# Attention and feed-forward block on one Trainium2 core: the first chunk's output product in half blocks, the third batch moved, the end's additions reordered

## The chip, the core and the metric

The kernel runs on one core of a Trainium2 chip. TensorE (PE) multiplies, VectorE (DVE), ScalarE (ACT) and GpSimd (POOL) work element by element, and DMAs are issued from the queues of SyncE (SP), ACT and POOL. POOL's queue holds its sums and the issues of all loads, in one order. The metric is device time: 554.34 us, the median of three runs (554.24 to 554.39).

## What is computed

For 8 batches, 8 heads, 1024 positions and 64 values a head, keys and values are first projected along the sequence to 64 rows; then attention, then a gated feed-forward layer on the 8192 rows of 512:

```
k_proj = einsum('ks,bhsd->bhkd', E, k);  v_proj = einsum('ks,bhsd->bhkd', F, v)
attn = softmax(q @ k_proj^T / 8);        x = attn @ v_proj, heads side by side: 8192 x 512
out  = (silu(x @ w_gate) * (x @ w_val)) @ w_out          # 512 -> 1536 -> 512
```

## The kernel before, in words

The 8192 rows are 16 chunks of 512, two for each batch. The main loop (L849) has 192 iterations t = 12 c + f: chunk c, block f of 128 of the 1536 inner columns. An iteration is `f_g` (four matmuls of 512 columns, ACT's tanh), `f_v` (four more, and two operations on DVE that leave a block of hT, the inner activations), then what the table `late` holds for t. Around them run two *slots*, 2t behind `f_g` and 2t+1 behind the rest of the iteration. The dictionary `slots`, written out by hand in `place` (L651) and around it, puts the attention of the coming batches there. Every engine works in the order in which this code issues, so the tables set the order on PE, ACT, DVE, POOL and SP alike.

The steps of the attention of batch b, by their short names:

- `load_q`, `load_k`, `load_v`: DMAs from POOL's queue, float32 to bf16; q in two halves (ch 0 and 1). Within a slot the loads go first (L826).
- `u_KV` (or `u_K1`, `u_V1` for batch 1): the projections, PE into tile kvp, then copies. `u_KT`: keys transposed into the tile BD. `u_V1` and `u_KT` copy on DVE.
- `u_TD`: a transposing DMA on SP, qTd from qb. `u_S`: scores sc from qTd and BD (L353), exp on ACT into ee. `u_R`: sums and reciprocals on DVE. `u_N`: POOL divides, AAd from ee and rr (L383).
- `u_AD`: a transposing DMA on SP, AT from AAd (L338). Four `u_N` make one AAd. `u_PV`: pv from AT (L410), copied to xT, the feed-forward's input.

For batch 1 the scores stand in slots 35 to 38 and 41 to 44, `u_AD` in 41 and 47, the first four `u_PV` in 44, 45, 46 and 46. For batch 2 `u_KV` stands in slot 56, the first `u_TD` in 57, the scores in 62, 65 and so on to 83; its loads are issued in slots 43 (K, V), 44 and 45 (the halves of q). Later batches have the same steps at other distances.

The output product hT x w_out of a chunk has two forms. Chunk 0 uses the plain one, `f_y` (L492): 4 x 12 matmuls of 512 columns, in twelve parts laid into iterations 16 to 23. Chunks 1 to 15 use seven products of half blocks (Strassen-Winograd style), `f_m` (L604): for each of two row groups p seven products m = 3, 4, 5, 2, 1, 6, 7 of six matmuls of 256 columns, from sums of quarters of hT (`h_sum`, tiles hs1 to hs7) and of w_out (`w_sum`, tiles ws1 to ws7, made once). Their results are put together by `m_34` (ACT copies to xs, POOL adds into tt), `m_52` (ACT copies to ysb), `m_16` (DVE adds, POOL subtracts, L594) and `m_7` (DVE adds, SP stores). hs5 and hs2 are summed on POOL, block by block, in the second half of each chunk; hs1, hs6 and hs7 on DVE, in one operation each (L547, 128x1536) in the next chunk; the five `w_sum` on DVE in iterations 18 to 22.

PSUM banks come from rings of two (a, g, v) and two single banks y and z. While `ring["wide"]` is true (chunks 0 and 1) the attention's ring a takes bank z as a third one.

The last chunk has its own ending, `f_m_last` (L616): products 3, 6 and 4 of both row groups, then 5 and 2 with three DVE operations after each, then products 1 of both (into banks z1[0], z1[1]) and products 7 into the same banks, which DVE must have emptied by L640 before.

Of the kernel before, what the change touches and what calls it, by code (L numbers as in the profile page):

```python
# [10 lines left out]
ALU = mybir.AluOpType  # L11
AX = mybir.AxisListType
BF16 = mybir.dt.bfloat16
FP32 = mybir.dt.float32
# [6 lines left out]
DM = H * D  # L21
DFF = 1536
P = 128
# [3 lines left out]
NFT = DFF // P  # L27
# [11 lines left out]
def kernel(  # L39
# [155 lines left out]
    def u_V1(b, at="a"):  # L195

        t = bank(at, [P, NPAIR, D], FP32, "kvp")
        src = vb[b][:].rearrange("p (a c) j d -> p a c j d", c=2)
        for j in range(NJ):
            for c in range(2):  # L200
                nc.tensor.matmul(
                    out=t[64 * c : 64 * c + 64],
                    lhsT=FT[:, j, :],
                    rhs=src[:, :, c, j, :],
                    start=(j == 0),
                    stop=(j == NJ - 1),
                )
        for c in range(2):
            rows = slice(64 * c, 64 * c + 64)
            nc.vector.tensor_copy(out=BDV[b % 2][rows, :, rows], in_=t[rows])  # L210

    def u_V0(p0, p1, at):

# [42 lines left out]
    def u_KT(b, at="a", prs=(0, NPAIR)):  # L256

        t = bank(at, [P, NPAIR, KP], FP32, "kTp")
        for pr in range(*prs) if b > 1 else ():
            nc.tensor.matmul(
                out=t[:, pr, :],
                lhsT=ks[b % 2][:, 2 * pr : 2 * pr + 2, :].rearrange("p h d -> p (h d)"),
                rhs=ident_bf[:, 0:KP],
                start=True,
                stop=True,
            )
        for g in range(2) if b < 2 else ():  # L270
            turn_ksp(t, b, g)
        bd = BD[b % 2][:].rearrange("p (a c) k -> p a c k", c=2)
        for c in range(2):
            src = t[64 * c : 64 * c + 64, slice(*prs)]
            nc.vector.tensor_copy(out=bd[0:64, slice(*prs), c, 0:64], in_=src)
            nc.vector.tensor_copy(out=bd[64:128, slice(*prs), c, 64:128], in_=src)

    def u_KT0(prs, ats, engs):

# [207 lines left out]
            out=hT[c][:, f, :], in0=s1[:], scalar=0.5, in1=ps[:], op0=ALU.mult, op1=ALU.mult  # L487
        )

    yy = {}  # L490

    def f_y(c, n):  # L492

        i, part = divmod(n, 3)
        if part == 0:
            yy[c] = bank("y", [P, DM], FP32, "yps")
        for f in range(4 * part, 4 * part + 4):
            nc.tensor.matmul(
                out=yy[c][:],
                lhsT=hT[c][:, f, i * P : (i + 1) * P],  # L500
                rhs=wo[:, f, :],
                start=(f == 0),
                stop=(f == NFT - 1),
            )
        if part == 2:
            ysb = y_pool.tile([P, 2, DM], FP32, name="ysb", tag="ysb")
            nc.scalar.copy(out=ysb[:, 0], in_=yy[c][:])
            nc.sync.dma_start(out=rows_of(c)[:, i, :], in_=ysb[:, 0])

    def rows_of(c):  # L510
        b, ch = divmod(c, CH)
        return out[b * S : (b + 1) * S, :].rearrange("(p c j) d -> p c j d", c=CH, j=4)[:, ch]

    def quarter(t, half, x):
        return t[:, HF * half : HF * (half + 1), HC * x : HC * (x + 1)]

    def w_sum(m):

        (a, b), op = {
            1: (((0, 0), (1, 1)), ALU.add),  # L520
            3: (((0, 1), (1, 1)), ALU.subtract),
            4: (((1, 0), (0, 0)), ALU.subtract),
            6: (((0, 0), (0, 1)), ALU.add),
            7: (((1, 0), (1, 1)), ALU.add),
        }[m]
        nc.vector.tensor_tensor(out=ws[m][:], in0=quarter(wo, *a), in1=quarter(wo, *b), op=op)

    hs = {}

# [86 lines left out]
    def f_m_last(c):  # L616

        xx[c, 0], xx[c, 1] = m_bank("y"), m_bank("g")
        z6 = m_bank("a")
        z1 = [m_bank("av"[p]) for p in range(2)]  # L620
        for p in range(2):
            m_mm(c, p, 3, xx[c, p][:, 0], start=True)
        for p in range(2):
            m_mm(c, p, 6, z6[:, p], start=(p == 0))
        for p in range(2):
            m_mm(c, p, 4, xx[c, p][:, 1])
            m_34(c, p)
        for p in range(2):
            m_mm(c, p, 5, xx[c, p][:, 0])
            m_mm(c, p, 2, xx[c, p][:, 1])  # L630
            m_52(c, p)
            d, ysb = tt[c, p], yo[c, p]
            nc.vector.tensor_tensor(out=d[:, 1], in0=d[:, 0], in1=ysb[:, 2], op=ALU.subtract)
            nc.vector.tensor_tensor(out=d[:, 0], in0=d[:, 0], in1=ysb[:, 1], op=ALU.subtract)
            nc.vector.tensor_tensor(out=d[:, 1], in0=d[:, 1], in1=z6[:, p], op=ALU.add)
        for x in (1, 0):
            for p in range(2):
                m_mm(c, p, (7, 1)[x], z1[p][:, 0], start=(x == 1))
                ysb = yo[c, p]
                nc.vector.tensor_tensor(out=ysb[:, 3 * x], in0=tt[c, p][:, x], in1=z1[p][:, 0], op=ALU.add)  # L640
                (nc.sync, nc.scalar)[p].dma_start(
                    out=rows_of(c)[:, p + 2 * x, :], in_=ysb[:, 2 * x : 2 * x + 2].rearrange("p x d -> p (x d)")
                )


    slots = defaultdict(list)

    def put(s, fn, *a):
        slots[s].append((fn, a))

    def place(b):  # L651
        s0 = 48 * (b - 1)
        if b == 1:
            put(22, u_TD, 1, 0)
            put(29, u_K1, 1)
            put(32, u_KT, 1)
            put(40, u_V1, 1)
            sa = (35, 36, 37, 38, 41, 42, 43, 44)
            put(41, u_AD, 1, 0)
            put(30, u_TD, 1, 1)  # L660
            put(47, u_AD, 1, 1)
            sp = (44, 45, 46, 46, 66, 67, 68, 69)
        else:
            put(s0 + (8 if b == 2 else 0), u_KV, b)
            put(s0 + (11 if b == 2 else 3), u_KT, b)
            o = 14 if b == 2 else 6
            put(s0 + (9 if b == 2 else -6), u_TD, b, 0)
# [16 lines left out]
    with tc.manual_schedule():  # L684
# [131 lines left out]
            place(b)  # L816
        for b in range(2, B):
            s0 = 48 * (b - 1) - (20 if b == 3 else 24)
            at = (43, 43, 44, 45) if b == 2 else (s0, s0 + 2, s0 + 4, s0 + 6)
            put(at[0], load_k, b)  # L820
            put(at[1], load_v, b)
            put(at[2], load_q, b, 0)
            put(at[3], load_q, b, 1)
# [3 lines left out]


        late = defaultdict(list)
        for n in range(NFT):  # L830
            late[NFT + 4 + (2 * n + 1) // 3].append((f_y, 0, n))
        for m, f in ((3, 6), (4, 7), (6, 8), (7, 9), (1, 10)):
            late[NFT + f].append((w_sum, m))
        for c in range(1, NC):
            for f in range(HF):
                for m in (5, 2):
                    late[c * NFT + HF + f].append((h_sum, c, m, f, f + 1))
            if c == NC - 1:
# [51 lines left out]
```

## Time and profile before

| | |
|---|---|
| median of three runs | 554.34 us |
| the profiled execution's own time | 554.06 us |
| its span, first to last instruction | 552.3 us |
| PE busy | 537.3 us (97%) |
| DVE, POOL, ACT busy | 414.1, 294.5, 233.3 us |
| 512-column matmuls of f_g and f_v | some 190 us each |
| POOL's half sums hs, 128x256 (L547) | x180, 120.6 us, mean 691 ns |
| DVE's sums hs (L547), 128x1536 for the most part | x49, 46.1 us, mean 946 ns |
| loads: q half, K, V, issue to landing | median 18.1, 9.9, 14.8 us |
| transposing DMAs qTd and AT, issue to landing | median 6.0 and 4.2 us |

The profile is of one execution, so the times of single instructions are set against 554.06 and 552.3, not against the median. "x" is the number of instructions. Matmuls overlap: a duration of 379 ns for 512 columns holds the tail of the pipeline, while the next one starts 216 ns after. A wait of PE is named by what ended it. An idle engine other than PE costs nothing by itself; it does if PE, later, waits for what it makes.

### The profile page before, as it was taken

The page shows a single profiled execution, that of the slowest core. Times are in us where ns is not written, and L with a number is a line of the kernel's source. Part 1 is how long each engine was busy: PE and PEld are TensorE (multiplying, and loading weights), DVE is VectorE, ACT ScalarE, POOL GpSimd, SP SyncE. Part 2 cuts the span into 40 slices and gives each one's busy share as a digit, 9 for nine tenths or more (in the row PEclk, how much of TensorE's full clock was granted, in tenths as well). Part 3 has the DMA queues.
Part 4 walks back from the last instruction along what each step waited for, and adds up shares of the span by engine and source line. Part 5 has one row for each costly group of instructions (what it writes and reads, how often), then busy time and mean ns, then how long its engine had stood idle before and what let it go on. Part 6 is the DMA issues. An engine that isn't in the chain of part 4 may idle for free. (4 is left out here: it accounts for less than half of the span.)

```text
span 552.3 us, 9270 instructions
## 1 busy us (share of the span) xinstructions
PE 537.3 (97%) x3438; PEld 317.9 (58%) x3500; DVE 414.1 (75%) x699; ACT 233.3 (42%) x416; POOL 294.5 (53%) x364
## 2 busy tenths in 40 slices
PE   7999999999999999999999999999999999999996
PEld 4654545566565655566556655566656565555565
DVE  3787896878597875979579785788859786676883
ACT  3564453353445333443425434344244533433331
POOL 7851493467617934377534855268461763526171
PEclk9999999999999999999999999999999999999999
DMA  9999969929932598038941299214990212110013
GB/s 205 192 197 190 162 142 194 160 72 139 211 76 73 104 189 170 1 77 145 206 108 39 64 170 195 71 39 92 179 209 17 74 47 72 39 40 31 8 39 115
DMA packets 111630, 62.87 MB, mean 114 GB/s; under 512 B 65888, under 2 KB 102752, under 8 KB 111584
## 3 DMA queue, kind: packets, MB, share of 16 engines
q0 software_dynamic: 43952, 29.49, 37.5%
q1 hardware_dynamic: 66800, 31.20, 25.4%
q10 hardware_dynamic: 832, 1.57, 0.9%
q8 instruction: 27, 0.44, 0.3%
q14 instruction: 19, 0.16, 0.1%
HBM read 60.29 MB, written 16.78 MB: 140 GB/s over the span
## 5 line engine op out<-in xcount | busy, mean ns | idle before, releaser
L462 PE MATMUL vps<-xT,wv 128*128 128x512 bf16 (+1 forms) x759 | 195.0, 377 | 2.5 <-DMA wv<-in_moe_w_val_dram 0.8
L462 PE MATMUL gps<-xT,wg 128*128 128x512 bf16 (+1 forms) x729 | 191.6, 377 | 1.9
L474 ACT ACTIVATE th<-gps 128x512 f32<-128x512 f32 x191 | 114.1, 598 | 164.7 <-PE gps L462 153.9
L481 DVE SCALAR_TENSOR_TENSOR s<-th,gps 128x512 f32<-128x512 f32 x191 | 129.2, 676 | 67.5 <-ACT th L474 66.2
L547 POOL TENSOR_TENSOR hs<-hT 128x256 bf16<-128x256 bf16 x180 | 120.6, 691 | 57.9 <-DVE hT L486 57.2
L486 DVE SCALAR_TENSOR_TENSOR hT<-s,vps 128x512 bf16<-128x512 f32 x192 | 132.1, 688 | 20.4 <-PE gps L462 0.5
L462 PEld LDWEIGHTS <-wv 128*128 128x128 bf16 x776 | 73.9, 98 | 84.3 <-issue 3.0
L564 PEld LDWEIGHTS <-hs 128*128 128x128 bf16 x900 | 88.0, 98 | 36.7 <-issue 3.3
L462 PEld LDWEIGHTS <-wg 128*128 128x128 bf16 x776 | 74.1, 98 | 55.9 <-issue 0.6
L383 POOL TENSOR_TENSOR AAd<-ee,rr 128x512 bf16<-128x512 f32 x56 | 58.4, 1043 | 55.7 <-issue 33.6
L594 POOL TENSOR_TENSOR tt<-tt,ysb 128x512 f32<-128x512 f32 x28 | 35.5, 1268 | 71.7 <-DVE tt L593 71.7
L564 PE MATMUL yps<-ws,hs 128*128 128x256 bf16 x540 | 68.6, 272 | 1.5 <-DVE ysb L640 1.2
L583 POOL TENSOR_TENSOR tt<-xs 128x256 f32<-128x256 f32 x30 | 29.4, 981 | 51.3 <-ACT xs L581 51.2
L150 ACT CAST xT<-pv 128x512 bf16<-128x512 f32 (+1 forms) x63 | 36.4, 581 | 46.3 <-PE pv L410 44.3
L368 DVE TENSOR_REDUCE zz<-ee 128x8 f32<-128x512 f32 x64 | 43.3, 677 | 11.1 <-ACT ee L357 11.0
L564 PE MATMUL yps<-ws,hT 128*128 128x256 bf16 x360 | 48.8, 273 | 0.0
L564 PE MATMUL yps<-wo,hs 128*128 128x256 bf16 x360 | 48.6, 273 | 0.1
L547 DVE TENSOR_TENSOR hs<-hT 128x1536 bf16<-128x1536 bf16 (+1 forms) x49 | 46.1, 946 | 0.1
L357 ACT ACTIVATE ee<-sc 128x512 f32<-128x512 f32 x64 | 38.1, 598 | 18.5 <-PE sc L353 16.1
L564 PEld LDWEIGHTS <-hT 128*128 128x128 bf16 x360 | 35.2, 98 | 16.0
L581 ACT COPY xs<-yps 128x512 f32<-128x512 f32 x30 | 17.6, 585 | 30.6 <-PE yps L564 30.5
L588 ACT COPY ysb<-yps 128x512 f32<-128x512 f32 x30 | 17.6, 585 | 24.9 <-PE yps L564 21.6
(100 smaller groups left out, 318.0 us busy)
## 6 DMA issues: line engine op xcount, KB each, us to landing
out_dram<-ysb SPq DMA_DIRECT2D x28, 512.0 KB, 2.7
qb<-in_q_dram POOLq DMA_DIRECT2D x14, 512.0 KB, 18.1
kb<-in_k_dram POOLq DMA_DIRECT2D x7, 1024.0 KB, 9.9
vb<-in_v_dram POOLq DMA_DIRECT2D x7, 1024.0 KB, 14.8
wo<-in_moe_w_out_dram POOLq DMA_DIRECT2D x2, 768.0 KB, 21.4
out_dram<-ysb SPq DMA_DIRECT2D x6, 256.0 KB, 2.2
kraw<-in_k_dram ACTq DMA_DIRECT2D x2, 512.0 KB, 4.8
qb<-in_q_dram POOLq DMA_DIRECT2D x4, 256.0 KB, 7.9
```

The lines of the kernel that those rows point to most:

```text
L150: (nc.scalar.copy if eng is nc.scalar else eng.tensor_copy)(out=out, in_=in_)
L357: nc.scalar.activation(out=e[:].rearrange("p h j k -> p (h j k)"), in_=ps[:].rearrange("p a k -> p (a k)"), func=AF.Exp, scale=scale,)
L368: nc.vector.reduce_sum(out=z[:], in_=e[:], axis=AX.X)
L383: eng.tensor_tensor(out=a.rearrange("p j h k -> p h j k"), in0=ee.pop((b, u))[:], in1=rr.pop((b, u))[:].unsqueeze(3).to_broadcast([P, 4, 2 ...
L462: nc.tensor.matmul(out=ps[:, ts], lhsT=(wg, wv)[w][:, kt, f * P : (f + 1) * P], rhs=x[:, kt, ts], start=(kt == 0), stop=(kt == NKT - 1),)
L474: nc.scalar.activation(out=th[:], in_=ps[:], func=AF.Tanh, scale=0.5)
L481: nc.vector.scalar_tensor_tensor(out=s1[:], in0=th[:], scalar=1.0, in1=g[:], op0=ALU.add, op1=ALU.mult)
L486: nc.vector.scalar_tensor_tensor(out=hT[c][:, f, :], in0=s1[:], scalar=0.5, in1=ps[:], op0=ALU.mult, op1=ALU.mult)
L547: eng.tensor_tensor(out=hs[c, m][:, fs, :], in0=quarter(hT[c], *a)[:, fs], in1=quarter(hT[c], *b)[:, fs], op=op,)
L564: nc.tensor.matmul(out=ps, lhsT=lhsT, rhs=ws[m][:, f, :] if rhs is None else rhs, start=(start and f == 0), stop=(f == HF - 1), skip_group ...
L583: nc.gpsimd.tensor_tensor(out=t[:, 0], in0=xs[:, 0], in1=xs[:, 1], op=ALU.add)
L594: nc.gpsimd.tensor_tensor(out=t[:], in0=t[:], in1=yo[c, p][:, 1:3], op=ALU.subtract)
```

## The change

Four things are changed together.

1. Chunk 0 takes the seven products too; `f_y` goes. The fourteen parts stand in iterations 18 to 23, two or three in each. Their sums go to three engines: hs5 and hs2 block by block on POOL in iterations 6 to 11; hs6 on POOL in 12, hs1 on DVE in 13, hs7 on POOL in 14. The sum ws6 is made on POOL in iteration 15, ws3, ws4, ws1 and ws7 on DVE in 16, 17, 18 and 20. Bank z leaves the attention's ring from iteration 19 on (before, from 24).
2. Batch 2's steps from `u_KV` to the last score and the last `u_AD` come two slots later (its `u_TD` and `u_PV` stay). Its loads are issued in slots 40 (first half of q), 42 (K), 43 (V) and 45 (second half).
3. The copies of `u_V1`, and for batch 1 those of `u_KT`, go from DVE to ACT.
4. In `f_m_last` the additions of z6 come ahead of products 5 and 2, and one of the four subtractions goes behind the additions that empty z1.

The diff, without the removed `f_y`:

```diff
@@ u_V1
-            nc.vector.tensor_copy(out=BDV[b % 2][rows, :, rows], in_=t[rows])
+            nc.scalar.copy(out=BDV[b % 2][rows, :, rows], in_=t[rows])
@@ u_KT
-            nc.vector.tensor_copy(out=bd[0:64, slice(*prs), c, 0:64], in_=src)
-            nc.vector.tensor_copy(out=bd[64:128, slice(*prs), c, 64:128], in_=src)
+            for lo in (0, 64):
+                copy(nc.scalar if b == 1 else nc.vector, bd[lo : lo + 64, slice(*prs), c, lo : lo + 64], src)
@@ w_sum
-    def w_sum(m):
+    def w_sum(m, eng=nc.vector):
...
-        nc.vector.tensor_tensor(out=ws[m][:], in0=quarter(wo, *a), in1=quarter(wo, *b), op=op)
+        eng.tensor_tensor(out=ws[m][:], in0=quarter(wo, *a), in1=quarter(wo, *b), op=op)
@@ f_m_last
+        for p in range(2):
+            step(tt[c, p][:, 1], tt[c, p][:, 0], z6[:, p], add)
         for p in range(2):
             m_mm(c, p, 5, xx[c, p][:, 0])
             m_mm(c, p, 2, xx[c, p][:, 1])
             m_52(c, p)
-            d, ysb = tt[c, p], yo[c, p]
-            nc.vector.tensor_tensor(out=d[:, 1], in0=d[:, 0], in1=ysb[:, 2], op=ALU.subtract)
-            nc.vector.tensor_tensor(out=d[:, 0], in0=d[:, 0], in1=ysb[:, 1], op=ALU.subtract)
-            nc.vector.tensor_tensor(out=d[:, 1], in0=d[:, 1], in1=z6[:, p], op=ALU.add)
+        d, ysb = [tt[c, p] for p in range(2)], [yo[c, p] for p in range(2)]
+        step(d[0][:, 1], d[0][:, 1], ysb[0][:, 2], sub)
+        step(d[0][:, 0], d[0][:, 0], ysb[0][:, 1], sub)
+        step(d[1][:, 1], d[1][:, 1], ysb[1][:, 2], sub)
         for x in (1, 0):
             for p in range(2):
                 m_mm(c, p, (7, 1)[x], z1[p][:, 0], start=(x == 1))
-                nc.vector.tensor_tensor(out=ysb[:, 3 * x], in0=tt[c, p][:, x], in1=z1[p][:, 0], op=ALU.add)
+                step(ysb[p][:, 3 * x], d[p][:, x], z1[p][:, 0], add)
...
+            if x:
+                step(d[1][:, 0], d[1][:, 0], ysb[1][:, 1], sub)
@@ place
-            put(s0 + (8 if b == 2 else 0), u_KV, b)
-            put(s0 + (11 if b == 2 else 3), u_KT, b)
-            o = 14 if b == 2 else 6
+            put(s0 + (10 if b == 2 else 0), u_KV, b)
+            put(s0 + (13 if b == 2 else 3), u_KT, b)
+            o = 16 if b == 2 else 6
@@ loads of batch 2 (slots of K, V, q first half, q second half)
-            at = (43, 43, 44, 45) if b == 2 else (s0, s0 + 2, s0 + 4, s0 + 6)
+            at = (42, 43, 40, 45) if b == 2 else (s0, s0 + 2, s0 + 4, s0 + 6)
@@ late
-        for n in range(NFT):
-            late[NFT + 4 + (2 * n + 1) // 3].append((f_y, 0, n))
-        for m, f in ((3, 6), (4, 7), (6, 8), (7, 9), (1, 10)):
+        for m, f in ((3, 4), (4, 5), (1, 6), (7, 8)):
             late[NFT + f].append((w_sum, m))
-        for c in range(1, NC):
+        late[NFT + 3].append((w_sum, 6, nc.gpsimd))
+        for c in range(NC):
...
-                for i, m in enumerate((1, 6, 7)):
-                    late[(c + 1) * NFT + 1 + i].append((h_sum, c, m, 0, HF, nc.vector))
-                for n, f in enumerate((0, 1, 2, 3, 4, 4, 5, 6, 7, 8, 9, 10, 10, 11)):
+                for m, f, eng in ((6, 0, nc.gpsimd), (1, 1, nc.vector), (7, 2, nc.gpsimd)) if c == 0 else (
+                    (1, 1, nc.vector), (6, 2, nc.vector), (7, 3, nc.vector)
+                ):
+                    late[(c + 1) * NFT + f].append((h_sum, c, m, 0, HF, eng))
+                fs = (6, 6, 7, 7, 8, 8, 9, 9, 9, 10, 10, 11, 11, 11) if c == 0 else (0, 1, 2, 3, 4, 4, 5, 6, 7, 8, 9, 10, 10, 11)
+                for n, f in enumerate(fs):
                     late[(c + 1) * NFT + f].append((f_m, c, n))
@@ main loop
-            ring["wide"] = c < 2
+            ring["wide"] = t < NFT + 7
```

More of the change, by code (lines that the diff above doesn't have):

```diff
@@ L488, in f_v @@
         )
[L490 to L508, printed above, removed]
     def rows_of(c):
@@ L627, in f_m_last, with step @@
             m_34(c, p)
+        add, sub = ALU.add, ALU.subtract
+        def step(o, i0, i1, op):
+            nc.vector.tensor_tensor(out=o, in0=i0, in1=i1, op=op)
+        for p in range(2):
+            step(tt[c, p][:, 1], tt[c, p][:, 0], z6[:, p], add)
         for p in range(2):
@@ L638, in f_m_last @@
                 m_mm(c, p, (7, 1)[x], z1[p][:, 0], start=(x == 1))
-                ysb = yo[c, p]
-                nc.vector.tensor_tensor(out=ysb[:, 3 * x], in0=tt[c, p][:, x], in1=z1[p][:, 0], op=ALU.add)
+                step(ysb[p][:, 3 * x], d[p][:, x], z1[p][:, 0], add)
                 (nc.sync, nc.scalar)[p].dma_start(
-                    out=rows_of(c)[:, p + 2 * x, :], in_=ysb[:, 2 * x : 2 * x + 2].rearrange("p x d -> p (x d)")
+                    out=rows_of(c)[:, p + 2 * x, :], in_=ysb[p][:, 2 * x : 2 * x + 2].rearrange("p x d -> p (x d)")
                 )
+            if x:
+                step(d[1][:, 0], d[1][:, 0], ysb[1][:, 1], sub)
     slots = defaultdict(list)
```

## The prediction

> **What bounds the kernel.** Read first the busy shares, then what TensorE (PE) waits for, then its timeline at each place the change touches.
>
> ```profile
> PE 537.3 (97%) x3438; PEld 317.9 (58%) x3500; DVE 414.1 (75%) x699; ACT 233.3 (42%) x416; POOL 294.5 (53%) x364
> ```
> ```profile
> PE yps L564 <- DVE ysb L640: 1.2, 1, 1.2
> PE kvp L162 <- DMA vb<-in_v_dram: 0.9, 1, 0.9
> ...
> PE sc L353 <- DMA qTd<-qb: 0.4, 1, 0.4
> ```
>
> PE is the bound: after the first 30 us almost nothing holds it but these three waits (us in total, times, longest), and all three are edited. So each edit is worth what it does to PE's stream. Matmuls start 0.216 us apart at 512 columns (4 in 0.865) and 0.109 apart at 256 (12 in 1.31); a wait's real loss is a little more than the idle shown, because the last matmul's tail counts as busy.
>
> **The output product of chunk 0.** It removes 48 matmuls of 512 columns, 48 x 0.216 = 10.38 us, and adds 2 x 7 x 6 = 84 of 256, 84 x 0.109 = 9.17: on paper 1.21 us less. But it also moves them. Three parts of the old product (L498, 3 x 0.865 = 2.59 us) stood before the first score of batch 1; all the new ones stand behind it. Here is that score (sc), with the wait that the table doesn't show:
>
> ```profile
> 57.97 1.89 PE L498 MATMUL yps<-wo,hT 128*128 128x512 bf16 x8
> 59.70 0.39 PE L353 MATMUL sc<-BD,qTd 128*128 128x128 bf16 x4
> ```
> ```profile
> 40.69 27.23 SPq L331 DMA_TRANSPOSE qTd<-qb  x2
> ```
> ```profile
> DMA to landing us min/median/max: 18.8/18.8/18.8
> ```
>
> The transposing DMA that brings qTd was issued at 40.69 and landed 18.76 us later, at 59.45; the score started at 59.70. It had 0.25 us in hand. Its slowness is the DMA engines': from 45 to 58 us its queue (q1) and the loads' queue (q0, weights, then V) moved one packet each in turn.
>
> ```profile
> q0 software_dynamic: 1904, 1.92, 90.0%
> q1 hardware_dynamic: 1905, 0.49, 33.0%
> ```
>
> V of batch 1 is issued later in the changed kernel (POOL now has eight sums of chunk 0 before it, 44.3 for 42.3), but queues behind w_out, which lands only at 56.9, so the engines see the same work and qTd lands at about 59.45 again. PE, relieved of 2.59 us, is there at 57.1 and waits 2.4. So of this part the first 2.59 us gain only 0.2, and behind it stand 14 x 0.655 = 9.17 us where 9 x 0.865 = 7.78 stood: +1.39. **Net +1.2, a loss.** The longest gap that the trace has behind the start is 1.18 us, with the granted clock at 1.00 after it (545 to 552); it shows no gap of 2.4. The Trainium skill, "TensorE: Matmul & The Clock Gate" (Part 1, What's actually happening), halves PE's clock after an idle window of some 3.4 us: by it a 2.4 us gap costs itself alone, and one that filled a window an estimated 1.7 us more (3.4 us at half speed).
>
> That wait covers all that the change puts on POOL and ACT before it: 12 half sums (hs, 0.65 each when alone), of which those between the four AA products of batch 0 may hold PE's transposes at L399 some 0.2 us; ACT's four copies to BD (nearest row L193, 0.37 each, done by 57); DVE's first weight sums (0.95 each). On POOL three sums of 128x1536 follow from about 48.7. No row has one: bounds are 3.0 us (six times 256 elements at 0.65, less five starts of 0.17) and 5.8 (six at 0.97, the pace beside a DVE sum of two SBUF inputs, 1.94 for two at 63.43). I take 3.2, near the undisturbed row, as DVE has only three such sums here: done at 58.3, before the first AAd at 61.8; at 5.8 it would be 66.1. The Trainium skill's "GPSIMD Engine Reference" (4.1 Engine selection) has two-input operations at about twice VectorE's time, by which they would take an estimated 1.9 each.
>
> **The transposed attention of batch 1.** This step has little room, and two edits press on it. AAd's fourth product on POOL releases the transposing DMA (AT, L338), which the first pv needs:
>
> ```profile
> 69.59 1.05 POOL L383 TENSOR_TENSOR AAd<-ee,rr 128x512 bf16<-128x512 f32 x1
> ```
> ```profile
> DMA to landing us min/median/max: 4.2/4.2/4.2
> ```
> ```profile
> 75.31 0.39 PE L353 MATMUL sc<-BD,qTd 128*128 128x128 bf16 x4
> 75.53 0.38 PE L410 MATMUL pv<-AT,BDV 128*128 128x512 bf16 x1
> ```
>
> Issued at 70.67, landed at 74.91, used at 75.53: 0.6 us in hand. After the change PE gets to pv at 59.50 + 15.83 (as before) + 0.71 (nine parts of 0.655 for six of 0.865) = 76.04. POOL's chain: first AAd at 61.8, 2.3 behind the score (2.46 now, with a ysb copy ahead of ee on ACT) (1.04), one new tt (0.72 to 1.38, waits for PE's second product, 63.8), two hs (1.30), two AAd (2.04), two hs (1.30), the fourth AAd (1.04): 70.15, a little earlier than now, since the weight sums that slowed its hs (2.01 for 1.30) have moved. Alone AT would land at 74.4 with 1.6 us spare. But the same event now releases the load of q for batch 2, moved three slots up to just behind that AAd on POOL. Until now K came first, six us later. Bounds for AT: 4.24 (q's packets come too late to matter) and 7.3. The upper: a load's first packet comes about 2 us after its issue (K issued 76.70, first packets 78.84), when some 1000 of AT's 2080 are still to go at 835 per us (1270 in 1.5 us of 72.5 to 74.0); in turns with q's 1024 of 512 B both move at 240 per us, as here from 92 to 97:
>
> ```profile
> q0 software_dynamic: 1189, 0.61, 87.6%
> q1 hardware_dynamic: 1193, 0.31, 46.1%
> ```
>
> That is 1024 x (1/240 - 1/835) = 3.0 us longer. A load begins thinly, though: K moved 301 packets in 78.8 to 81.0, not the 440 of its later pace. So I take 6.2: landing at 76.4, a wait of 0.4, between 0 and 1.4 (4 if K's packets join too).
>
> **The third batch.** K and V of batch 2 meet their product (kvp) too early:
>
> ```profile
> 91.10 1.03 PE L462 MATMUL gps<-xT,wg 128*128 128x512 bf16 x4
> 92.06 0.40 PE L162 MATMUL kvp<-kb,ET 128*64 128x512 bf16 x1
> 93.33 0.38 PE L162 MATMUL kvp<-vb,FT 128*64 128x512 bf16 x1 [0.87 <-DMA vb<-in_v_dram]
> ```
>
> From the gps to the next vps 3.83 us pass here; in batch 3, without a wait, 2.60 (148.79 to 151.39): 1.24 lost. The first score likewise loses 0.57 (102.22 to 103.89, for 1.09 in batch 3). With q first, V lands about 92 as now (93.29), while the product, two slots (3 us) later and behind the 1.2 us above, comes at 96 or after; qTd, waiting for a q that is long there, lands about 100 and its score comes at 106. Both waits go: **-1.81**. What is late next: the second AT of batch 2, two slots later (136.2 becomes 139) and so among batch 3's loads (up to 15.8 us there), but its pv at slot 105 runs at 163.65 now; batch 3's qTd behind it on SP has 4.8 us before its score. No cost.
>
> **The end.**
>
> ```profile
> 544.08 1.47 PE L564 MATMUL yps<-ws,hs 128*128 128x256 bf16 x12
> 546.73 1.47 PE L564 MATMUL yps<-ws,hs 128*128 128x256 bf16 x12 [1.18 <-DVE ysb L640]
> ```
>
> The last two products wait for DVE to empty a bank; 1.35 us are lost (545.385 to 546.73). DVE's chain from 544.00 to that addition's end at 546.68 has seven operations at 0.33 to 0.47. Afterwards z6 is added in DVE's idle time (540.04 to 544.00) and one subtraction goes behind the bank's addition, so three stand before it; the third needs ACT's copy that ends at 544.86: 544.90, then the addition 545.24 to 545.65. PE goes on at 545.7: **-1.0** (no less than 0.6 if ACT's result reaches DVE 0.45 us late, as at 544.00; no more than 1.35). The stores keep their order behind it.
>
> **Sum.** +1.2 + 0.4 - 1.81 - 1.0 = -1.2 us. The profiled execution took 554.06 (span 552.3 and 1.76 around), 0.28 under the median 554.34: 552.9 by the one, 553.1 by the other. **I take 553.0.** About 0.2% (1.1 us) is what a measurement of this kernel can tell from no change: faster means under 553.2, slower over 555.45.
>
> **Rivals.** (1) AT shares the engines fully with q. Then PE waits 0.8 to 3 us at pv and the gain is spent: 553.4 to 555.4, no change. For it: the equal packet counts wherever two queues have work. Against: the thin start. The case that the edits to batch 2 or the end do less than they say (+1.24 or +0.4) lands in the same place.
> (2) Slower: POOL arrives late at the fourth AAd. With its three long sums at 5.8 us the chain ends at 73.6 instead of 70.15, AT lands at 77.9 alone and 80.9 beside q, pv waits 1.9 to 4.9: up to 557.6. It costs more than the rest brings (1.6) once AT lands after 77.7, and is measurably slower once it lands after 79.1, that is, once POOL is 1.6 us late and the sharing is full. For it: POOL's 2.01 us pair beside DVE. Against: DVE has few two-input sums there.
>
> **Chances.** Little wait at pv, 552.0 to 553.2: 50%. Rival 1: 30%. Rival 2, or a wait I don't see at the denser chunk 1: 20%. Faster 0.50, same 0.30, slower 0.20. Range 552.0 (end at its best, no wait at pv) to 555.8, which leaves out most of rival 2.
>
> **What would show it.** PE sc waiting about 2.4 us for DMA qTd near 57 to 59.5; no wait of kvp for vb; pv L410 waiting for AT between 0 and 1.4 us near 76; the gap before the last products about 0.2 instead of 1.18. I am wrong if qTd lands earlier than 59 (a gain of up to 2.4 more), if PE's clock drops after the gap, or if POOL's 128x1536 sums take over 4 us.

## The result, and the profile after

The changed kernel takes 559.81 us, the median of six runs (557.2 to 561.0); before takes 554.29 beside it. The ratio is 1.0098, with an interval of 1.0076 to 1.0119: **slower by 1%**. The forecast was 553.0, the range 552.0 to 555.8, so both the sign and the range were wrong. The ratios here and below leave out runs over 1.5% above the fastest of their kernel; the only one is the run of 561.51 with the filled wait.

The profile shown here is of the shortest of the six runs: 557.2 us, span 555.4, that is 3.14 us more than the profiled run of before (554.06). The other five take 559.65 to 561.0 and show a lower granted clock (the share of full speed at which TensorE ran, 0.990 to 0.994 on average for 1.000). So there are two things to find: 3.14 us that the trace of this run holds, and some 2.6 us more that it doesn't.

First the busy shares of the changed kernel, then its waits of TensorE (us in total, times, longest):

```profile
PE 540.8 (97%) x3536; PEld 321.2 (58%) x3536; DVE 415.2 (75%) x697; ACT 235.0 (42%) x422; POOL 314.0 (57%) x383
```
```profile
PE pv L410 <- DMA AT<-AAd: 3.5, 1, 3.5
PE sc L353 <- DMA qTd<-qb: 2.3, 1, 2.3
...
PE yps L545 <- DVE tt L574: 0.6, 1, 0.6
...
PE yps L545 <- DVE ysb L612: 0.2, 1, 0.2
```

The three waits of before are gone or short: no kvp, no score of batch 2, and 0.2 for 1.2 at the end. The score's wait of 2.3 was forecast. The first row was forecast as 0.4, and the third not at all. PE's timeline shows where they stand (start, duration, and in brackets the idle time and what ended it):

```profile
56.59 1.03 PE L462 MATMUL vps<-xT,wv 128*128 128x512 bf16 x4
59.87 0.40 PE L353 MATMUL sc<-BD,qTd 128*128 128x128 bf16 x4 [2.25 <-DMA qTd<-qb]
...
76.21 0.39 PE L353 MATMUL sc<-BD,qTd 128*128 128x128 bf16 x4
80.13 0.39 PE L410 MATMUL pv<-AT,BDV 128*128 128x512 bf16 x1 [3.54 <-DMA AT<-AAd]
...
84.93 1.47 PE L545 MATMUL yps<-ws,hs 128*128 128x256 bf16 x12
86.98 0.82 PE L545 MATMUL yps<-ws,hs 128*128 128x256 bf16 x6 [0.58 <-DVE tt L574]
```

Without its wait pv would follow the score after 0.22 us, at 76.43; it starts at 80.13. The two DMA rows behind it are SP's issue of AT and, from the view of the tile AT, its time from issue to landing (4.2 before). SP's issue itself takes 3.17 us; the third row is that of before, 1.93:

```profile
70.88 3.17 SPq L338 DMA_TRANSPOSE AT<-AAd  x1
```
```profile
DMA to landing us min/median/max: 9.2/9.2/9.2
```
```profile
L338 SPq DMA_TRANSPOSE AT<-AAd x1: 1931/1931/1931, 70.7 to 70.7; - x1
```

POOL was in time. Its second and third sum of 128x1536, the AAd that releases AT, and the load of q just behind it:

```profile
51.76 3.81 POOL L528 TENSOR_TENSOR hs<-hT 128x1536 bf16<-128x1536 bf16 x1
55.54 3.08 POOL L507 TENSOR_TENSOR ws<-wo 128x1536 bf16<-128x1536 bf16 x1
...
69.81 1.04 POOL L383 TENSOR_TENSOR AAd<-ee,rr 128x512 bf16<-128x512 f32 x1
70.79 0.94 POOL L116 DMA_DIRECT2D qb<-in_q_dram  x1
```

Of the three sums that I put at 3.2 two take 3.1 and one, at 51.76, takes 3.81. The third ends at 58.62 (forecast 58.3), and AAd at 70.85 where I had 70.15. So AT is not issued late; it is slow on its way. Of AT's 2048 packets so many move from 72 to 73.5 us, in the changed kernel and then in before (a row holds a queue, its packets, MB, and their share of the engines' time; q1 carries SP's DMAs, q0 POOL's loads):

```profile
q1 hardware_dynamic: 697, 0.18, 73.5%
```
```profile
q1 hardware_dynamic: 1262, 0.32, 117.2%
```

Both rows hold AT alone: no other queue has a row there. With q's load issued just ahead of it (70.79), AT moves 465 packets per us for 841, before any packet of q's. q's packets begin at 73.53, and from 74.5 to 77.5 the two queues of the changed kernel move

```profile
q0 software_dynamic: 543, 0.28, 78.4%
q1 hardware_dynamic: 709, 0.18, 67.2%
```

that is 181 and 236 per us. AT's packets take 6.47 us (72.04 to 78.51) for 2.59 (71.83 to 74.42), and it counts as landed 1.57 us behind the last of them, for 0.5: +3.9 and +1.1, which is the 5.0 between 4.24 and 9.2. K, issued at 74.63, has no part in it here: its first packet (1 KB; q's have 512 B) moves at 78.72, behind AT's last.

At the end it went as forecast. PE's last product waits 0.15 (before, 1.18), for DVE's additions:

```profile
548.36 1.47 PE L545 MATMUL yps<-ws,hs 128*128 128x256 bf16 x12
549.99 1.47 PE L545 MATMUL yps<-ws,hs 128*128 128x256 bf16 x12 [0.15 <-DVE ysb L612]
```

**Where the 3.14 us of the profiled run are:** start-up +0.35 (the first gate matmul at 28.26 for 27.91, ahead of everything the change touches); chunk 0's product +1.2 (-0.2 ahead of the score, +1.39 behind it); pv +3.70; the wait at 86.98 +0.74; batch 2's two waits -1.81; the end -1.0. Sum: +3.2.

### The profile page after: what moved, and what is told of

Same layout as the page of the kernel before. It is cut to its first block, busy times and chain, and to the rows that moved or that the text cites. A ratio compares the mean times of both kernels' runs of the same rounds, so it can differ in the third digit from the quotient of the medians.

```text
span 555.4 us, 9421 instructions
## 1 busy us (share of the span) xinstructions
PE 540.8 (97%) x3536; PEld 321.2 (58%) x3536; DVE 415.2 (75%) x697; ACT 235.0 (42%) x422; POOL 314.0 (57%) x383
## 3 DMA queue, kind: packets, MB, share of 16 engines
q10 hardware_dynamic: 832, 1.57, 0.9%
## 4 chain that ended last, share of the span: by engine, by line
PE 76%; DMA 10%; DVE 10%; POOL 2%; issue 1%; ACT 1%; DVEq 0%; POOLq 0%; ACTq 0%
PE gps L462 24%; PE vps L462 23%; PE yps L545 23%; DMA qTd<-qb 3%; DVE hs L528 2%; DVE s L481 2%; PE pv L410 2%; DMA qb<-in_q_dram 2%; PE kvp L162 2%; DVE hT L486 2%; PE sc L353 2%; DMA AT<-AAd 2%; DMA Fraw<-in_F_dram 1%; DVE BD L150 1%; DMA wv<-in_moe_w_val_dram 1%
## 5 line engine op out<-in xcount | busy, mean ns | idle before, releaser
L462 PE MATMUL vps<-xT,wv 128*128 128x512 bf16 (+1 forms) x776 | 197.5, 377 | 0.8 <-DMA wv<-in_moe_w_val_dram 0.8
L462 PE MATMUL gps<-xT,wg 128*128 128x512 bf16 (+1 forms) x772 | 196.5, 377 | 0.0
L528 POOL TENSOR_TENSOR hs<-hT 128x256 bf16<-128x256 bf16 (+1 forms) x194 | 132.4, 704 | 60.3 <-DVE hT L486 59.4
L545 PEld LDWEIGHTS <-hs 128*128 128x128 bf16 x960 | 93.9, 98 | 38.2 <-issue 3.0
L383 POOL TENSOR_TENSOR AAd<-ee,rr 128x512 bf16<-128x512 f32 x56 | 58.3, 1042 | 46.2 <-issue 33.4
L575 POOL TENSOR_TENSOR tt<-tt,ysb 128x512 f32<-128x512 f32 x30 | 38.1, 1268 | 66.4 <-DVE tt L574 66.0
L545 PE MATMUL yps<-ws,hs 128*128 128x256 bf16 x576 | 73.2, 272 | 1.0 <-DVE tt L574 0.6
L564 POOL TENSOR_TENSOR tt<-xs 128x256 f32<-128x256 f32 x32 | 31.4, 982 | 52.0 <-ACT xs L562 51.8
L545 PE MATMUL yps<-ws,hT 128*128 128x256 bf16 x384 | 51.7, 273 | 0.0
L545 PE MATMUL yps<-wo,hs 128*128 128x256 bf16 x384 | 51.6, 273 | 0.1
L545 PEld LDWEIGHTS <-hT 128*128 128x128 bf16 x384 | 37.6, 98 | 16.5
```

The source lines that it names most:

```text
L383: eng.tensor_tensor(out=a.rearrange("p j h k -> p h j k"), in0=ee.pop((b, u))[:], in1=rr.pop((b, u))[:].unsqueeze(3).to_broadcast([P, 4, 2 ...
L462: nc.tensor.matmul(out=ps[:, ts], lhsT=(wg, wv)[w][:, kt, f * P : (f + 1) * P], rhs=x[:, kt, ts], start=(kt == 0), stop=(kt == NKT - 1),)
L528: eng.tensor_tensor(out=hs[c, m][:, fs, :], in0=quarter(hT[c], *a)[:, fs], in1=quarter(hT[c], *b)[:, fs], op=op,)
L545: nc.tensor.matmul(out=ps, lhsT=lhsT, rhs=ws[m][:, f, :] if rhs is None else rhs, start=(start and f == 0), stop=(f == HF - 1), skip_group ...
L564: nc.gpsimd.tensor_tensor(out=t[:, 0], in0=xs[:, 0], in1=xs[:, 1], op=ALU.add)
L575: nc.gpsimd.tensor_tensor(out=t[:], in0=t[:], in1=yo[c, p][:, 1:3], op=ALU.subtract)
```

## The experiments

The **theory** after this result: AT shares the DMA engines with the load of q, which the change moved in front of it, and lands 5 us later; what the usual runs lose beyond that is PE's clock, which falls to half behind a wait of two or three microseconds. The **rivals**: the load of K, issued at 74.63, takes part in AT's delay; the denser chunk 1 (more matmuls, more sums on POOL) makes AT or PE late by itself; the lower clock belongs to the run or to the denser work, and not to the waits. Letters in the expectations are explained where they stand; their short names are e1 for the loads put back, e2 for before with the loads moved, e3 for K and V later, e4 for the shift and the new end, f1 for e1 with the wait filled.

### Only the loads put back

```diff
-            at = (42, 43, 40, 45) if b == 2 else (s0, s0 + 2, s0 + 4, s0 + 6)
+            at = (43, 43, 44, 45) if b == 2 else (s0, s0 + 2, s0 + 4, s0 + 6)
```

> The changed kernel, with the loads of batch 2 issued in the slots they had before (K and V in 43, q in 44 and 45); all else stays changed. Theory A: q's load beside the transposing DMA of AT makes pv wait 3.7 us, and that wait is also what lowers PE's clock in most runs. Then pv doesn't wait, the score's wait of 2.25 us and the 0.7 us before the last product of chunk 0 stay, the time is 557.2 - 3.7 = 553.5 (553 to 554) and the clock 1.00 in every run. Theory B: AT is late because POOL has more to do, and the clock falls because of the score's wait. Then pv still waits 2 us or more, most runs have a clock of 0.99, and the time is 557 to 560.

Ten runs: median 558.18, from 553.52 to 559.33; ratio 1.0051 [1.0026, 1.0077]. In the trace (a run of 555.14) AT lands 4.24 us after its issue and pv doesn't wait (the row is that of the tile AT): with q back behind it, AT's delay is gone, though all the sums and matmuls of the change are there.

```profile
DMA to landing us min/median/max: 4.2/4.2/4.2
```

But the run is not at 553.5, and its clock is not whole, as Theory A had it; the table of stretches shows why. Its columns are the stretch, its length, the busy time of PE, PEld, DVE, ACT and POOL with their counts, PE's granted clock, the DMA share, and GB/s:

```profile
57.00:59.90 2.90, 0.69 (x5) 0.18 (x4) 2.58 (x3) 0.56 (x1) 1.60 (x1) 1.00 1.23 199
59.90:62.00 2.10, 2.10 (x13) 1.17 (x14) 2.00 (x4) 0.87 (x2) 0.00 (x0) 0.60 1.29 204
62.00:64.00 2.00, 2.00 (x9) 0.86 (x7) 1.17 (x4) 0.81 (x2) 1.04 (x1) 0.56 1.43 195
64.00:66.00 2.00, 2.00 (x19) 1.50 (x17) 2.00 (x3) 0.81 (x2) 0.14 (x1) 1.00 0.18 23
```
```profile
59.82 0.40 PE L353 MATMUL sc<-BD,qTd 128*128 128x128 bf16 x4 [2.21 <-DMA qTd<-qb]
60.05 1.64 PE L462 MATMUL gps<-xT,wg 128*128 128x512 bf16 x4
61.48 0.63 PE L353 MATMUL sc<-BD,qTd 128*128 128x128 bf16 x4
61.91 1.91 PE L462 MATMUL vps<-xT,wv 128*128 128x512 bf16 x4
```

Behind the score's wait of 2.21 us the clock is at half from 60.33 for 3.41 us; four matmuls that take 1.03 us take 1.91. Half of 3.41 is lost, 1.7 us. So the score's wait alone can lower the clock, without a wait at pv.

The same kernel was run three times more, for a trace of a run without that stretch and of one of 558 to 559 us.

> e1_loads_back itself, one more trace, hoped to be one of its runs of 558 to 559. Theory C: a wait of pv for AT near 138 us, batch 2's first AT landing more than 12 us after its issue. Theory D: no such wait; the clock stays at half for 6.8 or 10.2 us behind the score's wait. In a run of 553.5 to 555.3: neither.

> The same kernel as e1_loads_back once more, to see a run of 558 to 559 us, if it comes up. Theory C: its AT of batch 2 lands late beside batch 3's K, and its first pv of batch 2 waits 2 us or more. Theory D: no wait is longer than in the other run and PE has more stretches of half clock. A run of 555.2 us with one stretch near 60 us tells nothing new.

> The same kernel as e1_loads_back once more, to see a run of 558 to 559 us, if it comes up. Theory C: its AT of batch 2 lands late beside batch 3's K, and its first pv of batch 2 waits 2 us or more. Theory D: no wait is longer than in the other run and PE has more stretches of half clock. A run of 555.2 us with one stretch near 60 us tells nothing new.

They took 555.25, 553.49 and 555.03. The first and third show the same stretch of 3.41 us; the second has the same wait, and no stretch:

```profile
59.84 0.40 PE L353 MATMUL sc<-BD,qTd 128*128 128x128 bf16 x4 [2.21 <-DMA qTd<-qb]
60.08 1.03 PE L462 MATMUL gps<-xT,wg 128*128 128x512 bf16 x4
```

So one stretch makes the 1.6 us between 553.5 and 555.1. A run like six of the first ten (557.9 to 559.3) came up in none of the three; what holds those up stays open. The clock on record for each says that it is not the clock alone: the run of 557.9 has 0.997 on average, which leaves some 3.3 us at half clock, an estimate from 0.003 x 2 x 556. Half of that is lost, 1.7 of the 4.4 us above 553.5.

### The changed kernel once more

> The changed kernel itself, for a trace of one of its usual runs (five of six took 559.7 to 561, the one with the trace 557.2). Theory A: the trace shows PE's clock at half for one or more stretches of 3.4 us, begun just behind the wait at the score or at pv, and the time above 557.2 is the work done in those stretches at half speed: 1.7 us for each. Theory B: the clock is whole and a transfer or a wait elsewhere is longer.

This run took 559.96, one of the usual ones. Its waits of PE and two of its stretches:

```profile
PE pv L410 <- DMA AT<-AAd: 3.1, 1, 3.1
PE sc L353 <- DMA qTd<-qb: 2.3, 1, 2.3
```
```profile
62.00:64.00 2.00, 2.00 (x9) 1.09 (x8) 1.78 (x5) 0.17 (x1) 1.04 (x1) 0.50 1.36 185
...
82.00:84.00 2.00, 2.00 (x8) 0.95 (x7) 0.59 (x1) 0.29 (x1) 0.85 (x1) 0.50 1.16 271
```

The clock is at half for 3.41 us behind each of the two waits. Each costs 1.7; pv waits 0.4 less, because PE comes later. 557.2 + 1.7 + 1.7 - 0.4 = 560.2, for 559.96 measured. This is the difference between the profiled run and a usual one; the other usual runs have no trace, but clocks like this one's (0.990 to 0.994 for its 0.994).

### The changed kernel, with the score's wait filled

Eleven matmuls whose result nobody reads take PE's time ahead of the score of batch 1; they add work where PE would wait.

```diff
+        def fill(n):
+
+            ps = bank("y", [P, CW], FP32, "fill")
+            for _ in range(n):
+                nc.tensor.matmul(
+                    out=ps[:], lhsT=ident_bf[:], rhs=wo[:, 0, :], start=True, stop=True
+                )
+
+        slots[35].insert(0, (fill, (11,)))
```

> The changed kernel, with 11 unread matmuls of 512 columns (11 x 0.216 = 2.4 us) into the free bank y ahead of batch 1's first score, where PE waits 2.25 us for qTd; AT's loads stay as changed. Theory B (a wait of some 2 us is enough to halve the clock in most runs): the half-clock stretch near 61 us goes (a gain of 1.7 us where it was), the one behind pv's wait near 81 us stays: pv waits 3.1 to 3.7 us, 557 to 559 us in all. Rival (the stretches belong to the denser work and not to the waits): a stretch near 61 us stays, 559.5 to 561 us.

Median 559.14 (558.4 to 559.5); ratio 1.0094 [1.0077, 1.0111]. The trace (558.4): one long wait is left, and one stretch, behind it.

```profile
PE pv L410 <- DMA AT<-AAd: 3.6, 1, 3.6
```
```profile
62.00:64.00 2.00, 2.00 (x20) 1.54 (x18) 1.86 (x5) 0.74 (x2) 1.12 (x2) 1.00 1.35 183
...
79.00:81.00 2.00, 1.11 (x3) 0.44 (x4) 0.00 (x0) 0.46 (x1) 1.98 (x3) 0.56 1.21 256
81.00:83.00 2.00, 2.00 (x10) 1.08 (x9) 0.75 (x2) 0.12 (x1) 0.23 (x1) 0.58 1.23 222
```

The matmuls of the first stretch (20 for 9 above) run at full clock: here the filled wait brings no half clock, with the dense work behind it unchanged. One trace alone would prove little, since three of the eight traces with this wait escape too; but none of the four traces with the wait filled (this one and three further down) has the stretch. The median lies just above the 557 to 559 that were expected.

### Before, with only the loads of batch 2 moved

```diff
-            at = (43, 43, 44, 45) if b == 2 else (s0, s0 + 2, s0 + 4, s0 + 6)
+            at = (42, 43, 40, 45) if b == 2 else (s0, s0 + 2, s0 + 4, s0 + 6)
```

> The kernel before, with nothing changed but the slots of batch 2's loads (q 40, K 42, V 43, q 45). Theory A: AT is issued at 70.7 as now, takes 9.2 us instead of 4.2, pv waits 4.4 us; the two waits of batch 2 (1.8 us) go, as PE comes later and V earlier: 554.3 + 4.4 - 1.8 = 556.9 in a run that keeps its clock, 559 to 560 in one that doesn't, and most don't. Theory B: the loads' slots cost nothing, the two waits shrink: 552.5 to 554.3, clock 1.00.

Median 559.38 (558.67 to 561.55); ratio 1.010 [1.0078, 1.0121]. One line, without the new product, loses as much as the whole change. In its trace (561.55) AT takes 11.5 us, more than in the changed kernel; why more stays open. The view of AT, PE's wait and the stretches:

```profile
DMA to landing us min/median/max: 11.5/11.5/11.5
```
```profile
PE pv L410 <- DMA AT<-AAd: 6.5, 1, 6.5
```
```profile
77.00:82.00 5.00, 0.00 (x0) 0.00 (x0) 2.03 (x5) 0.00 (x0) 3.38 (x4) 0.56 1.40 189
82.00:85.00 3.00, 2.88 (x7) 1.04 (x8) 0.52 (x1) 0.59 (x1) 0.00 (x0) 0.50 1.24 215
85.00:88.00 3.00, 3.00 (x9) 1.08 (x8) 1.83 (x4) 0.59 (x1) 2.75 (x3) 0.52 1.24 207
```

The clock is at half for 10.24 us, three times 3.413, of which 5.8 are matmul time after the wait (82.1 to 87.9): 2.9 us more. The product of chunk 0 is not what makes AT late: it isn't in this kernel.

### The changed kernel, with K and V of batch 2 later

```diff
-            at = (42, 43, 40, 45) if b == 2 else (s0, s0 + 2, s0 + 4, s0 + 6)
+            at = (45, 45, 40, 45) if b == 2 else (s0, s0 + 2, s0 + 4, s0 + 6)
```

> The changed kernel with the first half of q still in slot 40, but K and V of batch 2 in slot 45. Theory A: AT shares the engines with q alone and then has them for itself: 7.3 to 8 us from issue to landing for 9.2, pv waits about 2 instead of 3.5, the clock stays 1.00 in most runs; V lands near 99 and kvp may wait up to 1 us: 555 to 556.5. Theory B: as the changed kernel, pv waits 3.5, 557 to 560.

Median 560.91 (559.83 to 566.11); ratio 1.0142 [1.0086, 1.0199]. From the view of AT, and the waits:

```profile
DMA to landing us min/median/max: 9.2/9.2/9.2
```
```profile
PE pv L410 <- DMA AT<-AAd: 3.2, 1, 3.2
```

The same 9.2 us without K. The expectation had AT quicker once K was away; it missed, and the first rival falls: the first half of q is enough. The run of 566.11 has no trace, and what made it so long stays open.

### Before, with only the shift of batch 2 and the new end

The steps of batch 2 stand two slots later and the end's additions are reordered, as in the change; loads, product and copies are those of before. The part on batch 2:

```diff
-            put(s0 + (8 if b == 2 else 0), u_KV, b)
-            put(s0 + (11 if b == 2 else 3), u_KT, b)
-            o = 14 if b == 2 else 6
+            put(s0 + (10 if b == 2 else 0), u_KV, b)
+            put(s0 + (13 if b == 2 else 3), u_KT, b)
+            o = 16 if b == 2 else 6
```

> The kernel before (chunk 0 with the plain product, loads in their old slots) with batch 2 two slots later and the new order of additions at the end. By both theories the two waits of batch 2 (1.8 us) and 1.0 to 1.2 us at the end go, and no wait at pv or at batch 1's score appears: 554.3 - 2.9 = 551.4 (551 to 552), clock 1.00. If moving batch 2 has a cost of its own (its second AT among batch 3's loads), it is over 552.

Median 551.65 (551.46 to 552.02); ratio 0.9954 [0.9940, 0.9969]: 2.5 us faster than the runs of before beside it (554.13). Of the waits that the two edits aim at, its trace (552.02) keeps only the 0.2 at the end. The first score of batch 2, at 104.71, doesn't wait; the 0.5 that this trace has for qTd is at 60.18, ahead of the first score of batch 1:

```profile
60.18 0.40 PE L353 MATMUL sc<-BD,qTd 128*128 128x128 bf16 x4 [0.50 <-DMA qTd<-qb]
...
104.71 0.39 PE L353 MATMUL sc<-BD,qTd 128*128 128x128 bf16 x4
```
```profile
PE yps L564 <- DVE ysb L631: 0.2, 1, 0.2
```

The two edits bring nearly the 2.8 us that the prediction gave them (1.81 + 1.0), with the loads in their old order. The gain on batch 2 needed the two slots, not q first.

### The loads put back, the score's wait filled; then the late product spaced too

The first is the kernel with only the loads put back, with the eleven unread matmuls. The second also takes the products 12 and 13 of the fourteen (m = 1 and 6 of the second row group) into iteration 22, so that only m = 7 is left in iteration 23 (its expectation names only m = 6; the edit moves both):

```diff
-                fs = (6, 6, 7, 7, 8, 8, 9, 9, 9, 10, 10, 11, 11, 11) if c == 0 else (0, 1, 2, 3, 4, 4, 5, 6, 7, 8, 9, 10, 10, 11)
+                fs = (6, 6, 7, 7, 8, 8, 9, 9, 9, 10, 10, 10, 10, 11) if c == 0 else (0, 1, 2, 3, 4, 4, 5, 6, 7, 8, 9, 10, 10, 11)
```

> As e1_loads_back, and where PE waits for batch 1's qTd (slot 35, ahead of the first score) it gets 11 matmuls of 512 columns that nobody reads, 2.4 us, into the bank that is free then. PE ends no piece of useful work earlier or later by them. Theory A (an idle PE of 2.2 us is enough for its clock to fall to half, for one or several stretches of 3.4 us): with PE busy the clock stays at 1.00, and every run takes what the best of e1 took, 553.5 (553 to 554.2), where e1 had 553.5 to 559.3 and a median of 558.2. Theory B (the slow runs of e1 come from something else, the transfers or POOL): the median stays at 557 to 559 and the runs stay spread.

> f1_filled_wait itself, one more trace, hoped to be like the two of ten that took 560.0 and 561.5. Theory C: batch 2's first AT (slot 77) lands more than 12 us after its issue and pv waits near 138 us. Theory D can't be, since no score waits here. In a usual run: 553.1 to 553.8 and no such wait.

> As f1_filled_wait, and of chunk 0's last three products one (m = 6 of the second row group) goes from iteration 23 to 22, so that DVE has read product 1's bank before product 7 adds to it. The wait of PE yps for DVE tt (0.6 us of idle, 0.74 lost) goes: f1's time less 0.7, 552.8. If this wait is hidden behind another, the time stays f1's.

The first: median 553.60 of ten runs, eight of them 553.14 to 554.79, two at 560.03 and 561.51; ratio 1.0005 [0.9979, 1.0031]; and 553.32 once more. With PE kept busy the half-clock stretch is gone, at the same landing of qTd. Against 555.0 to 555.25 with the stretch that is 1.6 us, against 553.49 without it, nothing. No trace caught a run of 560; its clock (0.996) leaves an estimated 4.5 us at half clock, which costs 2.2 of its 6.5 us above 553.5, so it has some longer wait.

The second: median 552.61 (552.39 to 553.3); ratio 0.9973 [0.9962, 0.9983]. The wait of yps for tt, 0.6 in the first, has left the list: 1.0 us less by the medians, 0.85 without the two long runs of the first, for 0.7 expected. PE's timeline at the score:

```profile
57.40 2.54 PE L818 MATMUL fill<-wo,ident_bf 128*128 128x512 bf16 x11
59.83 0.40 PE L353 MATMUL sc<-BD,qTd 128*128 128x128 bf16 x4
```

Against the kernel with only the shift and the new end (551.65), this one has the new product of chunk 0 and the copies on ACT, at its best: about 1 us more, for the 1.2 that the prediction took. The two come from different groups of runs and their intervals overlap, so the 1 us is not sure.

### The attention's steps of batch 2 two slots later still

The fourth experiment's kernel (shift and end), with

```diff
-            o = 16 if b == 2 else 6
+            o = 18 if b == 2 else 6
```

> As e4_shift_and_end, with batch 2's scores and AT two slots later still (66 to 87, second AT at 91), so that qTd has landed: the wait of 0.5 us at the first score of batch 2 goes, 551.65 - 0.5 = 551.1. If the second AT now comes too late for its pv or holds batch 3's qTd on SP, 552 or more.

A miss, and it aimed at the wrong place: the wait of 0.5 us that the expectation puts at batch 2's first score stands at batch 1's, as shown above. Median 560.69 (560.12 to 560.8); ratio 1.0116 [1.0101, 1.0131]. The first AT of batch 2 is now issued at 124.15, just behind the loads of batch 3's K (122.11) and V (124.05); in the fourth experiment it was issued at 121.22, ahead of K (122.77), and landed after 4.3 us. The waits, the time from AT's issue to its landing, and the packets of the two queues from 127 to 142 us:

```profile
PE pv L410 <- DMA AT<-AAd: 6.5, 1, 6.5
```
```profile
DMA to landing us min/median/max: 18.5/18.5/18.5
```
```profile
q0 software_dynamic: 2423, 2.09, 93.0%
q1 hardware_dynamic: 2085, 0.55, 34.0%
```

By its trace it is the same mechanism in another place: 139 packets per us on AT's queue beside 162 of the loads, and the clock at half for 6.83 us from 141.04. No run took the loads out of the way with the steps left where they are.

### Batch 3's loads two slots later

To keep that place clear, batch 3's loads go two slots back, in the kernel with only the loads put back and in the one with the shift and the new end.

```diff
-            s0 = 48 * (b - 1) - (20 if b == 3 else 24)
+            s0 = 48 * (b - 1) - (18 if b == 3 else 24)
```

> As e1_loads_back, with batch 3's four loads two slots later (78 to 84 for 76 to 82). Open is why six of e1's ten runs took 558 to 559 when one half-speed stretch behind the score's wait explains only 555.2. Theory C: in the changed kernels batch 2's first AT is issued only 1.6 us ahead of batch 3's K (slots 77 and 76); when K comes a little earlier, AT takes 10 us or more instead of 4.3 and its pv waits at slot 87, with a drop of the clock behind it. Then with the loads later no run exceeds 555.5. Theory D: the stretches behind the score's wait are simply longer in some runs (two or three of 3.4 us). Then the runs still spread to 558 to 559.

> As e4_shift_and_end (plain product in chunk 0, batch 2 two slots later, new order at the end), with batch 3's four loads two slots later, so that batch 2's first AT has the engines for itself. Expected 551.6 (551.3 to 552.0) in every run, as e4, and no run above 553. If K of batch 3 then comes too late for its product, 552 or more.

The first: median 554.74 of ten (553.43 to 560.34), ratio 1.0029 [1.0002, 1.0056]. Three of ten runs take over 556 us for six of ten, which ten runs each can't tell apart, and no run over 555.5 was expected: batch 3's loads beside AT are at most a part of the runs that stay unexplained. The second: median 551.51 (551.4 to 552.6), ratio 0.9956 [0.9943, 0.9968], no other than without the edit. These two, **551.5 to 551.7 us, are the fastest versions**: before, with batch 2's steps two slots later and the end reordered. The kernel with the late product spaced (552.61) beats both kernels too.

## Why the prediction was wrong

The step that failed is "So I take 6.2: landing at 76.4, a wait of 0.4, between 0 and 1.4". AT took 9.2 and pv lost 3.7; the forecast's upper bound of 7.3 for AT, and Rival 1's 3 us at pv, were both too low. Rival 1 named the mechanism and had 30%; its price was too small, and it had no clock in it. Point by point:

- **AT beside q** (0.4 taken, 3.7 found). The sum assumed that AT runs at 835 packets per us until q's first packet, and that the two then move at 240 each until q's 1024 are through. In the trace AT is already at 465 before it, and here the sum failed: at 73.5, where q's packets begin, 565 fewer are through than in before. Beside q it then moves 270 per us to its end (1351 in 5.0 us), no slower than the 240 taken, so the 565 cost an estimated 2.1 us. "A load begins thinly" was true of q (33 packets in its first half microsecond) and no help, since AT had slowed as well. And the landing comes 1.57 us behind the last packet for 0.5, 1.1 us that the sum hadn't got. The two make 3.2 us, where 9.2 exceeds 6.2 by 3.0. The "4 if K's packets join too" came near the 3.7 by chance, as K didn't join. (q's first half went up four slots, from 44 to 40; the prediction says three.)
- **The clock** (nothing taken; 1.7 at each of the two waits in the usual runs). The prediction named the rule and let the row of 1.18 us speak for a gap of 2.4: "a 2.4 us gap costs itself alone", though it listed a clock that drops after the gap as a sign of being wrong. Loads-back runs with the stretch and without it differ by 1.6 us, and filling the wait removes the stretch. The Trainium skill, "TensorE: Matmul & The Clock Gate" (Part 1, What's actually happening), names half clock after at least one idle window of some 3.4 us, and a window that runs freely. The runs here agree on the length (3.413 us) and on its running freely; they differ on what counts as idle: 2.0 us without a matmul inside a window sufficed.
- **The wait at 86.98** (not seen; 0.74). Products 1, 6 and 7 of the second row group all stand in iteration 23. Product 7 adds into the half bank that `m_16`'s addition on DVE (L574) still reads after product 1, with only the six matmuls of product 6 between them. Taking two of the three into iteration 22 removed it. The prediction counted the parts and didn't look at which bank two neighbours use.
- **Chunk 0's product** (+1.2): right, as far as it was measured. The score's wait is 2.25 for 2.4, qTd lands at 59.82 for 59.45, and the version with this wait filled and the late wait removed stands 1.0 over the one with the old product.
- **POOL's sums** (3.2 taken, 3.1 found twice and 3.81 once) and its chain (70.15, 70.85): right, and Rival 2 didn't happen. The Trainium skill's "GPSIMD Engine Reference" (4.1 Engine selection) has such an operation at about twice VectorE's time, an estimated 1.9; the undisturbed row is 3.08, 3.2 times the 0.95 of DVE's.
- **Batch 2** (-1.81) and **the end** (-1.0): right, -2.5 together in a kernel of their own. The two stretches compared for kvp, 3.83 and 2.60, are 4.05 and 2.81 by the rows, with the same difference of 1.24. The prediction reckoned with q first; it wasn't needed.

The rest of the sum held: the forecast without its 0.4 for pv, and with the 0.74 that it didn't see, is 553.3, and the four traced runs with the loads put back, the late product not yet spaced and no half clock took 553.3 to 553.7.

What stays open: what the runs of 557.9 to 559.3 us with the loads put back, and of 560 to 561.5 with the filled wait, do differently, as no trace caught one; and why AT is slower before q's first packet moves. With q's load issued ahead of it SP's issue of AT takes 3.17 us for 1.93 (3.34 and 3.18 in the two other kernels with q first, 1.99 with the loads put back), so the slowing begins at the issue; the cause is not shown.

## What to carry to other kernels

A load that is moved up costs not its issue but the short DMA that is on the critical path beside it: look for what is in flight from its issue to its landing. Here that DMA slowed from the load's issue on, some 2.7 us ahead of the load's first packet, and was counted as landed later behind its last packet too. A wait on TensorE is not priced by its length alone: near 2 us it can bring 1.7 us more, in some runs and not in others, so the clock belongs in the sum and in the range, and a single profiled run may be the one without it. Move the steps that wait first and the loads only if a wait is left: here two slots took both of batch 2's waits away.

## What the runs showed of the hardware

**The clock follows free-running windows of 3.413 us.** In all seventeen traces, those of before and after among them, the changes of the granted clock lie on a grid of 3.413 us whose start differs from run to run. This is the count of the time without a matmul in a window of that grid at full clock, behind the start-up, wherever it is over 0.8 us:

```
idle in a window, us              clock of the next window
1.02 1.18 1.49 1.75 1.78 1.89 1.90 1.97    1.0
2.00 2.01 2.20 2.21 2.23 2.37 2.43 2.97 3.06 3.41    0.5
```

So the profiled run of the changed kernel was a lucky one: a border at 78.37 split its wait of 3.54 into 1.78 and 1.75, and one at 57.89 left 1.97 of the score's wait. With this bound a wait of 3.54 escapes only if the border leaves less than 2.0 on both sides, 0.46 of 3.41, an estimated 13% of runs; one of 2.25 escapes in about half (1.75 of 3.41). In a window that is already at half clock, 0.81, 1.07 and 1.63 us of idle time kept it there for another, and none let it go: the long waits pay twice or three times. The bound is read from traces and wasn't set by an experiment; idle time here counts the tails of matmuls as busy.

**A transposing DMA beside a load.** Issue to landing of AT, by what was issued just ahead of it: no load, 4.2 us; the first half of q, 9.2 in the changed kernel (with K behind it and without) and 11.5 in the kernel before, where K's packets begin at 78.51 with 1699 of AT's 2048 through; K and V of batch 3, 18.5. Where both queues have work for long they move packets in nearly equal numbers (1904 and 1905 in before from 45 to 58 us, 1189 and 1193 from 92 to 97), though those of the loads are larger (512 B or 1 KB for 256 B). That the tile's many small packets therefore decide how long it takes is an inference: no run changed their size.
